# Latencies of tiny DMAs in a planned kernel, earlier float64 conversion, and a float32 attention turned on TensorE

## The chip, the cores and the metric

The kernel runs on one core of a Trainium2 chip. The metric is the device time of one execution in microseconds. The core has TensorE (PE), VectorE (DVE), ScalarE (ACT) and GpSimd (POOL), each running its own instructions in order, and SyncE (SP), which here issues all DMAs, also in order.

## The reference

Clustered attention over 2 batches of 8 heads, 768 positions and 64 channels, then two feed-forward layers over 1536 tokens of 512 channels. All arithmetic of the reference is float32, except that the weights of the first layer, `w_in` and `w_out`, come as float64.

```python
q_assign = np.argmax(einsum('bhsd,hcd->bhsc', q_n, c_n), axis=-1)      # 16 clusters, normalised
k_assign = np.argmax(einsum('bhsd,hcd->bhsc', k_n, c_n), axis=-1)
scores = np.where(q_assign == k_assign, scale * q @ k.T, -1e9)
attn = softmax(scores); x = attn @ v                                   # to 1536 x 512
h = x @ w_in;  g = h * clip(h + 3, 0, 6) / 6;  x = g @ w_out           # 512 -> 2048 -> 512
for e in range(4):                                                     # 512 -> 1024 -> 512 each
    out += p[:, e:e+1] * (maximum(x @ w1[e], 0) @ w2[e])
```

## The kernel before

One batch (half of the tokens) after the other: attention of batch 0, Moe1 of batch 0 (`w_in`, `w_out`, four chunks of 512 hidden channels), Moe2 of batch 0 (`w1`, `w2`, eight chunks) with the attention of batch 1 mixed in, Moe1 of batch 1, Moe2 of batch 1. Every large product is made of half-precision parts: a float32 value is scaled and split into a high and a low float16 half, and three products (`mm3`, L903 to L905) stand for one.

Attention takes two heads at a time (a pair, 4 of them) and 256 queries at a time (a block, 3 per pair). For each 128 queries `scores` makes two products of the queries with the 768 keys (L760, L762), whose second adds the cluster mask; in batch 0 a filling product of `junk` (L758) goes ahead. DVE takes the row maximum (`ut`, L767), ACT the exponential `e` with its sum (L768). `sums` (L776, L777) gives the reciprocal, and `halves` makes the normalised high and low halves `p` on ACT, POOL and DVE (L782 to L791). A DMA (`pt<-p`, L725) turns them, and 18 pairs of float16 products with `vh` and `vl`, the halves of v (L699, L700), make `psv` (L738). ACT and DVE split it into x1h and x1l (L746, L747), the input of Moe1.

`conv_w` converts one chunk of `w_in` or `w_out` from float64 bits to float32 in four steps of 128x512 values. Each step loads 512 KB (`r64`), ACT takes an absolute value (L884), and DVE does L885 (limits, with the maximum), L887, L889 and L891 (shifts and joins of bits). `allmax` then finds the chunk's maximum: DVE reduces to one value per partition (`am`, L503), a DMA writes 128 values to DRAM (`mx<-am`, L506), a second DMA reads them back to all partitions (`bc<-mx`, L508), DVE reduces (L509). `split_w` scales by it and splits into `w` (ACT L808 and L811, POOL L812); the halves are written to DRAM (`hl`) for batch 1. `load_w` does the same for the float32 weights of Moe2, and `vmax` for v. There are 26 such pairs of DMAs. `allmax_pe` does it for activations by a transpose and a product on the PE.

The order of all instructions on all queues is made by a planner in the kernel itself. Each piece of work has an engine, a modelled duration and a due time (`prio`); `plan` goes through modelled time and places on each engine what could start first, then what is due first. A DMA's modelled time is 1.1 us plus its bytes at 360 GB/s, and 0.91 to 1.0 us more until another engine or another DMA may use it. `PAR` holds due times, engine choices and buffer counts. Pools of buffers open and close in groups: the attention's buffers of batch 0 (`g_a[0]`) must close before Moe1's conversion buffers and its second weight pool open. The four buffers of `wrca` and two of `r64a` serve the first chunk, those of `g_m[0]` the other seven.

## Time and profile before

| | us |
|---|---|
| median of 3 runs | 1231.6 (1228.99 to 1234.57) |
| the profiled execution | 1227.56, its span 1225.8 |
| PE busy | 967.3 (79%) |
| DVE busy | 815.6 (67%) |
| ACT busy | 581.4 (47%) |
| POOL busy | 406.4 (33%) |

The shares are means over stages of different kinds. Read the stages first, then the chain of waits in each, then who waits for whom. A stage in which the PE is busy nearly all the time at full clock can only become shorter by less work; in the others one looks for what the waiting engine stands in front of.

### The profile page before, as it was taken

The page shows a single profiled execution, that of the slowest core. Times are in us where ns is not written, and L with a number is a line of the kernel's source. Part 1 is how long each engine was busy: PE and PEld are TensorE (multiplying, and loading weights), DVE is VectorE, ACT ScalarE, POOL GpSimd, SP SyncE. Part 2 cuts the span into 40 slices and gives each one's busy share as a digit, 9 for nine tenths or more (in the row PEclk, how much of TensorE's full clock was granted, in tenths as well). Part 3 has the DMA queues.
Part 4 walks back from the last instruction along what each step waited for, and adds up shares of the span by engine and source line. Part 5 has one row for each costly group of instructions (what it writes and reads, how often), then busy time and mean ns, then how long its engine had stood idle before and what let it go on. Part 6 is the DMA issues. An engine that isn't in the chain of part 4 may idle for free.

```text
span 1225.8 us, 16019 instructions
## 1 busy us (share of the span) xinstructions
PE 967.3 (79%) x5567; PEld 560.6 (46%) x5567; DVE 815.6 (67%) x1644; ACT 581.4 (47%) x1061; POOL 406.4 (33%) x353
## 2 busy tenths in 40 slices
PE   3476773667779577757769677999999989999998
PEld 2355551334345234433435344565566545555554
DVE  9798856549636657745655366666978985665544
ACT  6467762544553344524536244444555454443332
POOL 3566850323551526545434244422000001111111
PEclk9677887798889788878889897999999999999999
DMA  9497798667532557986657295568333314332211
GB/s 270 88 200 136 152 193 237 210 128 192 117 109 76 195 49 160 168 113 166 177 88 192 48 170 102 165 140 182 133 104 103 104 35 138 103 104 70 69 36 52
DMA packets 216562, 161.50 MB, mean 132 GB/s; under 512 B 161505, under 2 KB 164833, under 8 KB 216481
## 3 DMA queue, kind: packets, MB, share of 16 engines
q1 hardware_dynamic: 216480, 160.48, 55.2%
q8 instruction: 43, 0.70, 0.2%
q14 instruction: 39, 0.31, 0.1%
HBM read 86.70 MB, written 31.47 MB: 96 GB/s over the span
## 4 chain that ended last, share of the span: by engine, by line
PE 38%; DMA 30%; DVE 19%; POOL 4%; issue 4%; ACT 4%; SPq 1%; POOLq 0%; ACTq 0%; DVEq 0%
DMA mx<-am 11%; DMA pt<-p 9%; PE psm L903 5%; PE psm L904 5%; PE psm L905 5%; PE psw L981 4%; PE psw L982 4%; PE psw L980 4%; DVE p L791 3%; DMA bc<-mx 3%; DMA wraw<-in_w 3%; PE psg L904 3%; PE psg L905 3%; PE psg L903 3%; PE psv L738 2%
## 5 line engine op out<-in xcount | busy, mean ns | idle before, releaser
L905 PE MATMUL psm<-w,h 128*128 128x512 f16 x384 | 148.3, 386 | 17.8 <-DVE h L1144 9.1
L903 PE MATMUL psm<-w,h 128*128 128x512 f16 x384 | 148.4, 386 | 10.3 <-DVE xv L527 6.3
L904 PE MATMUL psm<-w,h 128*128 128x512 f16 x384 | 148.0, 385 | 0.0
L1144 POOL TENSOR_TENSOR h<-t,h 128x384 f16<-128x384 f32 x32 | 29.1, 916 | 329.9 <-ACT h L1143 309.7
L768 ACT ACTIVATE e<-pss,ut 128x768 f32<-128x768 f32 x96 | 86.0, 897 | 103.1 <-DVE ut L767 35.2
L904 PEld LDWEIGHTS <-w 128*128 128x128 f16 x704 | 71.3, 101 | 118.1 <-issue 79.7
L903 PE MATMUL psg<-g,w 128*128 128x384 f16 x256 | 88.4, 345 | 42.0 <-DVE t L1050 21.3
L903 PE MATMUL psm<-x2h,w 128*128 128x384 f16 x288 | 98.8, 343 | 17.1 <-DVE oa L1169 16.8
L791 DVE SCALAR_TENSOR_TENSOR p<-e,ut,p 128x768 f16<-128x768 f32 x62 | 79.4, 1286 | 37.5 <-POOL p L789 30.8
L738 PE MATMUL psv<-pt,vh 128*64 128x256 f16 x576 | 61.0, 336 | 54.3 <-DMA pt<-p 46.2
L903 PEld LDWEIGHTS <-w 128*128 128x128 f16 x704 | 71.2, 101 | 71.1 <-issue 16.1
L905 PEld LDWEIGHTS <-w 128*128 128x128 f16 x704 | 71.4, 101 | 60.2 <-issue 17.0
L904 PE MATMUL psm<-x2l,w 128*128 128x384 f16 x288 | 98.0, 340 | 0.1
L905 PE MATMUL psm<-x2h,w 128*128 128x384 f16 x288 | 97.5, 339 | 0.0
L1144 DVE TENSOR_TENSOR h<-t,h 128x384 f16<-128x384 f32 x96 | 62.8, 655 | 50.5 <-ACT h L1143 50.4
L767 DVE TENSOR_REDUCE ut<-pss 128x1 f32<-128x768 f32 x96 | 90.0, 945 | 8.0 <-PE pss L762 7.7
L904 PE MATMUL psg<-g,w 128*128 128x384 f16 x256 | 88.2, 345 | 5.7 <-POOL g L1052 2.9
L812 POOL TENSOR_TENSOR w<-wraw,w 128x512 f16<-128x512 f32 x64 | 80.1, 1272 | 34.8 <-ACT w L811 34.3
L1169 DVE SCALAR_TENSOR_TENSOR oa<-psm,pq,oa 128x512 f32<-128x512 f32 x84 | 62.6, 745 | 41.5 <-PE psm L905 41.1
L905 PE MATMUL psg<-g,w 128*128 128x384 f16 x256 | 87.8, 343 | 0.7 <-POOL w L812 0.7
L789 POOL TENSOR_SCALAR p<-e,ut 128x768 f16<-128x768 f32 x49 | 49.1, 1003 | 109.9 <-DMA pt<-p 58.2
L760 PE MATMUL pss<-ka,qa 128*128 128x384 f32 x192 | 71.0, 455 | 10.4 <-ACT e L768 10.3
(191 smaller groups left out, 2317.0 us busy)
## 6 DMA issues: line engine op xcount, KB each, us to landing
wraw<-in_w SPq DMA_DIRECT2D x92, 256.0 KB, 4.5
hl<-w SPq DMA_DIRECT2D x64, 256.0 KB, 4.6
w<-hl SPq DMA_DIRECT2D x64, 256.0 KB, 3.2
r<-in_w_in SPq DMA_DIRECT2D x16, 512.0 KB, 5.2
r<-in_w_out SPq DMA_DIRECT2D x16, 512.0 KB, 6.5
nat<-in_nat SPq DMA_DIRECT2D x16, 384.0 KB, 5.3
raw<-in_qk SPq DMA_DIRECT2D x16, 384.0 KB, 5.1
hl_i<-w SPq DMA_DIRECT2D x16, 256.0 KB, 4.4
```

Of the source, the lines that this page charges most:

```text
L738: nc.tensor.matmul(ps[64 * q:64 * q + 64], vs[vi][:, q, t], pts[q][:, :, pi * NT + t], start=i == 0, stop=i == n - 1)
L760: nc.tensor.matmul(ps[:, f, 0:HS], qa[:, qs], ka[:, f * HS:f * HS + HS], start=True, stop=False)
L767: dve(S, p, lambda: nc.vector.tensor_reduce(out=nb(), in_=ps[:, :, 0:HS], axis=AX.XY, op=ALU.max, negate=True), [ps], [(tb, n)])
L768: act(S, p, lambda: nc.scalar.activation(out=e.t.rearrange("p (a b) -> p a b", a=2), in_=ps[:, :, 0:HS], func=AF.Exp, bias=nb(), scale=1.0 ...
L789: pool(S, p, lambda: nc.gpsimd.tensor_scalar(out=pp[:, j, 0], in0=e.t, scalar1=rs(), scalar2=1.0, op0=ALU.mult, op1=ALU.mult), [e, key], [ ...
L791: dve(S, p, lambda: nc.vector.scalar_tensor_tensor(out=pp[:, j, 1], in0=e.t, scalar=rs(), in1=pp[:, j, 0], op0=ALU.mult, op1=ALU.subtract) ...
L812: pool(512, p, lambda w=w, raw=raw: nc.gpsimd.tensor_tensor(out=w[:, 1], in0=raw.t, in1=w[:, 0], op=ALU.subtract), [raw, (w, 0)], [(w, 1)])
L903: nc.tensor.matmul(o_, ah, bh, start=i == 0, stop=False)
L904: nc.tensor.matmul(o_, ah, bl, start=False, stop=False)
L905: nc.tensor.matmul(o_, al, bh, start=False, stop=i == 3)
L1144: low = lambda e: e.tensor_tensor(out=h[:, 1], in0=t.t, in1=h[:, 0], op=ALU.subtract)
L1169: dve(512, p, lambda: nc.vector.scalar_tensor_tensor(out=oa[:, t], in0=ps.t, scalar=q, in1=oa[:, t], op0=ALU.mult, op1=ALU.add), [ps, qk], ...
```

## The change

1. `add`, `dve` and `dma` take a `lag`, which delays in the plan whoever uses the result. `allmax` gives 7.0 us to the `mx` DMA, 4.0 us to the `bc` DMA and 0.3 us to the small DVE reduction. For v (both batches) the maximum now crosses partitions on the PE, as `allmax_pe` did; that function is merged into `allmax`.
2. `conv_w` is no longer called by Moe1. All eight conversions are recorded with due times from 90 us on, one per 22 us; their buffers (3 of `r64`, 8 of `wrc`, 4 of `stg`) are in a group of their own that is open from the start. The halves are written to DRAM only, and Moe1 of batch 0 reads them back as batch 1 does. Scaling of these weights moves from ACT to POOL.
3. The attention of batch 0 keeps its exponentials in float32. `turned` scales `e` on POOL, transposes it on the PE in two groups of three 128x128 blocks, copies each group out of PSUM (four of five on ACT, one on DVE), and multiplies by v in float32: 6 pairs of products per block. x1h and x1l are scaled as they leave PSUM. There are no halves of p and v, no turning DMA and no filling product in this attention; it has two score buffers in PSUM, where there were three, and two for the transposes.

```diff
-    spc=0.0,
-    cv=0.0,
-    wse=dict(i="A", o="A", **{"1": "P", "2": "A"}),
+    spc=4.0,
+    wse=dict(i="P", o="P", **{"1": "P", "2": "A"}),
+    lr=0.3,
+    ld=(7.0, 4.0),
-    r64p=-11.808027221836664,
+    r64p=6.0,
-    fill=384,
+    fill=0,
+    cv0=90.0,
+    cvd=22.0,
+    cvb=(3, 8, 4),
...
-                x.ready = max(x.ready, end + self.LAT.get((t.eng, x.eng), 0.0) + (0.31 if t.cols < 0 else 0.0))
+                x.ready = max(x.ready, end + self.LAT.get((t.eng, x.eng), 0.0) + (0.31 if t.cols < 0 else 0.0) + t.lag)
...
-    p_s = [Pool("ps_sa", 3, g_pa, True), Pool("ps_sb", 2, g_ps, True)]
+    p_s = [Pool("ps_sa", 2, g_pa, True), Pool("ps_sb", 2, g_ps, True)]
+    p_tr = Pool("ps_ta", PAR["trh"], g_pa, True)
...
-    r64 = [Pool("r64a", 2, g_l0), Pool("r64b", 4, g_m[0])]
-    wrc = [Pool("wrca", 4, g_l0), Pool("wrcb", 9, g_m[0])]
+    p_r64, p_wrc, p_stg = (Pool(x, k, g_cv) for x, k in zip(("r64", "wrc", "stg"), PAR["cvb"]))
...
+    def allmax(am, n, inv, ki, unit, sc, ks, p, bits=False, pp=None):
+
+        dve(n, p, lambda: nc.vector.tensor_reduce(out=am[:, n:n + 1], in_=am[:, 0:n], axis=AX.X, op=ALU.max), [am], [(am, "r")], lag=G["lr"])
+        if pp is None:
...
+            dma(5e3, p, lambda: nc.sync.dma_start(out=dr.t.unsqueeze(1), in_=am[:, n:n + 1]), [(am, "r")], [dr], lag=G["ld"][0])
+            bc = Buf(p_bc, [128, 128], F32, "bc")
+            dma(65e3, p, lambda: nc.sync.dma_start(out=bc.t, in_=dr.t.partition_broadcast(128)), [dr], [bc], lag=G["ld"][1])
...
+        def turned(self, hp, blk, p, avp):
...
+                    e = self.scores(qa, qb, ka, kb, blk * BQ + j * 128, tb, 0, p(i))
+                    self.sums(tb, 1, p(i), 1.0)
+                    sc = lambda eng, e=e, tb=tb: eng.tensor_scalar(out=e.t, in0=e.t, scalar1=tb[:, 2:3], scalar2=1.0, op0=ALU.mult, op1=ALU.mult)
...
+                        pe(NT // nh * 0.109, p(i) + PAR["trp"], turn, [e], [ps], NT // nh * 128)
...
+                        if PAR["kt"][((blk * 4 + i) * nh + h) % len(PAR["kt"])] == "A":
+                            act(S // nh, p(i) + PAR["trp"], lambda src=src, dst=dst: nc.scalar.activation(out=dst(), in_=src(), func=AF.Copy), [ps], [key], ps=True)
+                        else:
+                            dve(S // nh, p(i) + PAR["trp"], lambda src=src, dst=dst: nc.vector.tensor_copy(out=dst(), in_=src()), [ps], [key])
...
+            def av(part):
+                for t in range(part * NT // parts, (part + 1) * NT // parts):
+                    for q in range(2):
+                        nc.tensor.matmul(ps[64 * q:64 * q + 64], vr[:, q, t], pts[q][:, :, t], start=t == 0, stop=t == NT - 1)
...
-            if self.b == 0:
-                conv_w(key, {"i": w_in, "o": w_out}[n][c], p, 0 if (n, c) == ("i", 0) else 1)
-            else:
-                again_w(key, p)
-                if n == "i" and self.wino(c):
-                    sums_w(key, lambda k: wscr[key[1:]][k], p)
+            again_w(key, p)
+            if n == "i" and self.wino(c):
+                sums_w(key, lambda k: wscr[key[1:]][k], p)
...
-            a0.block(hp, blk, lambda i, t0=when[hp, blk]: t0 + i * T_UNIT, G["ka"][hp][4 * blk:4 * blk + 4], G["xba"][3 * hp + blk], G["avp"])
+            a0.turned(hp, blk, lambda i, t0=when[hp, blk]: t0 + i * T_UNIT, G["avpa"])
+
+    for i in range(2 * NC1):
+        n, c = "io"[i % 2], i // 2
+        conv_w((0, n, c), (w_in, w_out)[i % 2][c], G["cv0"] + G["cvd"] * i)
```

On DVE, at the end of the first attention, the kernel before runs as follows (`x1l0` is the attention's last result, `am_2112` the maximum of the first chunk of `w_out`):

```order
L885 TENSOR_SCALAR wconv_2120,am_2112<-wconv_2120 128x512
L747 SCALAR_TENSOR_TENSOR x1l0_820<-psv_2029,x1h0_809 128x256
L891 SCALAR_TENSOR_TENSOR wconv_2110<-r64_2102,wconv_2110 128x512
L887 TENSOR_SCALAR wconv_2120<-wconv_2120 128x512
L885 TENSOR_SCALAR wconv_2133,am_2112<-wconv_2133 128x512
L889 SCALAR_TENSOR_TENSOR wconv_2120<-r64_2104,wconv_2120 128x512
L887 TENSOR_SCALAR wconv_2133<-wconv_2133 128x512
L891 SCALAR_TENSOR_TENSOR wconv_2120<-r64_2104,wconv_2120 128x512
```

Now the same place, with `am_2198` the maximum of the third chunk of `w_out` and `bc_2290` that of the third of `w_in`:

```order
L954 SCALAR_TENSOR_TENSOR wconv_2234<-r64_2177,wconv_2234 128x512
L948 TENSOR_SCALAR wconv_2298,am_2198<-wconv_2298 128x512
L950 TENSOR_SCALAR wconv_2298<-wconv_2298 128x512
L512 TENSOR_REDUCE am_2198<-am_2198 128x1
L952 SCALAR_TENSOR_TENSOR wconv_2298<-r64_2248,wconv_2298 128x512
L954 SCALAR_TENSOR_TENSOR wconv_2298<-r64_2248,wconv_2298 128x512
L764 SCALAR_TENSOR_TENSOR x1l0_783<-psv_2293,vm_67,x1h0_760 128x256
L1110 SCALAR_TENSOR_TENSOR t_2358<-t_2358,psg1_2278 128x384
L519 TENSOR_REDUCE wv_68<-bc_2290 128x1
```

The second of eight conversions was under way when the last `x1l0` was made; now it is the sixth, and its steps are done.

On SP, in the third stage, the kernel before issues one tiny pair per chunk of `w1` or `w2`, among the turning DMAs of the second attention:

```order
L506 DMA mx2252_218<-am_5280 128x1
L725 DMA_TRANSPOSE pt_5455<-p_5487 128x12x128
L508 DMA bc_5530<-mx2252_218 128x128
L725 DMA_TRANSPOSE pt_5536<-p_5517 128x12x128
L725 DMA_TRANSPOSE pt_5536<-p_5552 128x12x128
L506 DMA mx2294_223<-am_5475 128x1
L725 DMA_TRANSPOSE pt_5621<-p_5591 128x12x128
L508 DMA bc_5638<-mx2294_223 128x128
```

Now, at the same kind of place:

```order
L516 DMA mx2445_222<-am_5878 128x1
L886 DMA hl_150_218<-w_5922 128x1024
L893 DMA wraw_5955<-in_w1 128x512
L886 DMA hl_151_219<-w_5931 128x1024
L893 DMA wraw_5978<-in_w1 128x512
L886 DMA hl_152_220<-w_5938 128x1024
L893 DMA wraw_6006<-in_w1 128x512
L886 DMA hl_153_221<-w_6008 128x1024
L893 DMA wraw_6037<-in_w1 128x512
L584 DMA raw_6061<-in_qk 128x768
L584 DMA raw_6063<-in_qk 128x768
L518 DMA bc_6074<-mx2445_222 128x128
```

The `bc` stood two rows behind its `mx`; it stands 11 rows behind it, and the writes and loads of weights go between.

On the PE, in the first attention, the end of one group of scores and the start of a block's products with v stood like this before:

```order
L758 LDWEIGHTS ident_b_61
L758 MATMUL pss_736<-junk_62,ident_b_61 128x384
L760 MATMUL pss_736<-ka_514,qa_498 128x384 x2
L762 MATMUL pss_736<-kb_532,qb_509 128x384 x2
L738 LDWEIGHTS vh_593
L738 MATMUL psv_750<-pt_643,vh_593 64x256
```

Now, with `e` the exponentials that are turned and `vr` the float32 v:

```order
L755 MATMUL psv_716<-pt_599,vr_358 64x256
L755 MATMUL psv_716<-pt_679,vr_358 64x256
L739 MATMUL pst_756<-ident_60,e_650 128x128 x3
L739 MATMUL pst_763<-ident_60,e_650 128x128 x3
L823 MATMUL pss_769<-ka_482,qa_465 128x384 x2
L825 MATMUL pss_769<-kb_502,qb_476 128x384 x2
```

The filling product is gone, a score is followed by six transposes of an earlier row block, and v is read in float32.

## Rows read from the trace of the kernel before

**Rows 1.** Stage windows: us, busy us (count) of five engines, PE clock, DMA share.

```profile
0.00:195.60 195.60, 115.44 (x795) 87.26 (x796) 156.40 (x317) 120.67 (x205) 109.91 (x87) 0.80 0.84 179
27.40:195.60 168.20, 104.80 (x741) 81.70 (x741) 131.85 (x253) 103.02 (x182) 102.40 (x76) 0.77 0.83 159
45.00:110.00 65.00, 39.98 (x270) 31.17 (x270) 60.43 (x110) 41.59 (x73) 41.73 (x29) 0.71 0.83 161
195.60:396.50 200.90, 139.42 (x747) 76.73 (x747) 123.02 (x287) 94.68 (x166) 70.05 (x62) 0.87 0.55 148
396.50:862.00 465.50, 356.36 (x2044) 202.32 (x2043) 287.10 (x547) 204.57 (x380) 197.34 (x172) 0.89 0.67 142
862.00:1225.80 363.80, 356.05 (x1985) 194.28 (x1982) 249.11 (x496) 161.44 (x310) 29.07 (x32) 0.99 0.26 85
```

**Rows 2.** Chain that ended last, from 195.6 to 396.5, then 396.5 to 862.

```profile
by line: DMA mx<-am 32.4%; DMA bc<-mx 8.8%; issue 6.1%; DVE wconv L889 5.8%; DMA r<-in_w_in 5.5%; DVE wconv L891 5.1%; PE psg L904 4.5%; PE psg L905 4.4%; PE psg L903 4.2%; DMA r<-in_w_out 2.7%; DVE wconv L885 2.3%; ACT wconv L808 2.2%; DVE
by line: DMA pt<-p 18.3%; DMA mx<-am 14.3%; DMA wraw<-in_w 7.5%; issue 5.0%; PE psv L738 4.3%; PE psm L903 4.3%; PE psm L904 4.1%; PE psm L905 4.0%; DVE p L791 3.6%; DMA bc<-mx 3.1%; DMA qb<-so 2.7%; POOL p L784 2.0%; DVE am L839 2.0%; POOL
```

**Rows 3.** DMA issues: names, count, KB each, median us to landing.

```profile
bc<-mx SPq DMA_DIRECT2D x26, 64.0 KB, 4.8
mx<-am SPq DMA_DIRECT2D x26, 0.5 KB, 8.5
```

**Rows 4.** Waits: DVE's before 195.6, two of DVE's after it, SP's after 396.5.

```profile
DVE vm L509 <- DMA bc<-mx: 6.4, 1, 6.4
DVE wv L509 <- DMA bc<-mx: 41.7, 7, 9.8
DVE wconv L885 <- ACT wconv L884: 9.5, 3, 4.5
SPq L508 <- DMA mx<-am: 82.3, 14, 9.4
```

**Rows 5.** Timeline of the PE: start us, us, line, tiles, shapes, count.

```profile
75.25 0.85 PE L616 MATMUL psc<-raw,ct 128*32 128x384 f32 x8
...
433.01 0.49 PE L624 MATMUL psct<-ident,sc 128*128 128x128 f32 x3
433.34 0.33 PE L903 MATMUL psm<-x2h,w 128*128 128x384 f16 x1
```

**Rows 6.** Groups by line on DVE, 0 to 195.6: busy us, mean ns, idle.

```profile
L791 DVE SCALAR_TENSOR_TENSOR p<-e,ut,p 128x768 f16<-128x768 f32 x26 | 35.2, 1359 | 9.7 <-ACT p L787 6.4 <-POOL p L789 3.1
L889 DVE SCALAR_TENSOR_TENSOR wconv<-r,wconv 128x512 int32<-128x512 int32 x5 | 5.5, 1091 | 0.0
L887 DVE TENSOR_SCALAR wconv<-wconv 128x512 int32<-128x512 int32 x5 | 4.1, 812 | 0.1
L885 DVE TENSOR_SCALAR_CACHE_REDUCE wconv<-wconv 128x512 f32<-128x512 f32 x6 | 4.0, 673 | 6.7 <-ACT wconv L884 6.7
L891 DVE SCALAR_TENSOR_TENSOR wconv<-r,wconv 128x512 int32<-128x512 int32 x5 | 4.0, 792 | 0.0
```

**Rows 7.** The same from 195.6 to 396.5.

```profile
L889 DVE SCALAR_TENSOR_TENSOR wconv<-r,wconv 128x512 int32<-128x512 int32 x27 | 22.9, 853 | 0.1
L887 DVE TENSOR_SCALAR wconv<-wconv 128x512 int32<-128x512 int32 x27 | 12.5, 465 | 0.2
```

**Rows 8.** ACT's L990; PE's L738 (window 0 to 195.6) and L758.

```profile
L990 ACT ACTIVATE keep<-psw 128x384 f32<-128x384 f32 x20 | 9.8, 488 | 49.4 <-PE psw L982 49.4
0.00:195.60 195.60, 37.00 (x432) 0.80 0.84 179
L758 PE MATMUL pss<-junk,ident_b 128*128 128x384 bf16 x48 | 19.0, 395 | 34.6 <-ACT e L768 34.5
```

**Rows 9.** PE's waits, 195.6 to 396.5 (first), 396.5 to 862 (others).

```profile
PE psg L903 <- DVE t L1050: 32.3, 10, 9.7
PE psv L738 <- DMA pt<-p: 38.5, 10, 7.8
PE pss L762 <- DMA qb<-so: 15.0, 2, 7.6
```

More of the change, by code (lines that the diff above doesn't have):

```diff
@@ L55 @@
     parts=3,
-    ka=["APDPPDPDADPA", "PADPPAPAAPAP", "PPDPPDDAAPAA", "PDPDPDPDPPAD"],
+    avpa=-8.0,
+    kn="PPPPPP",
+    kt="AAAAD",
     kb="DDDP",
@@ L79 @@
     dpx=2,
-    fill=384,
+    fill=0,
+    trp=3.0,
+    trh=2,
+    parta=6,
+    cv0=90.0,
+    cvd=22.0,
+    cvb=(3, 8, 4),
     wo1=0,
@@ L127 @@
 class Task:
-    __slots__ = ("eng", "dur", "fn", "prio", "n", "deps", "succ", "bufs", "ready", "idx", "dma", "cols", "tab", "name", "new", "end")
+    __slots__ = ("eng", "dur", "fn", "prio", "n", "deps", "succ", "bufs", "ready", "idx", "dma", "cols", "tab", "name", "new", "end", "lag")
 class Order:
@@ L155, in group, with add @@
         return g
-    def add(self, eng, dur, prio, fn, reads=(), writes=(), dma=0.0, cols=0, tab=None):
+    def add(self, eng, dur, prio, fn, reads=(), writes=(), dma=0.0, cols=0, tab=None, lag=0.0):
         t = Task()
-        t.cols, t.tab = cols, tab
+        t.cols, t.tab, t.lag = cols, tab, lag
         t.name = (writes[0][0] if isinstance(writes[0], tuple) else writes[0]).name if writes else "out"
@@ L362, in body @@
     NMB = S // MB
+    G = PAR
     o = Order(tc)
@@ L396, in body @@
     g_pf = o.group("psum", after=(g_ps,), keep=True)
-    g_m[0] = o.group("left", after=(g_a[0], g_l0))
+    g_m[0] = o.group("left", after=(g_a[0],))
     g_p0 = o.group("right")
@@ L534, in __init__ @@
             self.b = b
-            self.xb = max(PAR["xba"]) if b == 0 else PAR["xbb"]
-            prep = ("raw", "nat", "vr", "sc", "so", "cs", "oh", "sm")
+            self.xb = PAR["xbb"]
+            prep = ("raw", "nat", "sc", "so", "cs", "oh", "sm") + (("vr",) if b else ())
             P = lambda name: Pool(name + str(b), n[name], gp if name in prep else g)
-            self.p = {k: P(k) for k in ("raw", "nat", "vr", "sc", "so", "cs", "oh", "sm", "e", "p", "pt", "vh", "vl", "tiny")}
+            self.p = {k: P(k) for k in n if k != "stk"}
             if b == 0:
@@ L691, in vmax @@
             k = [(vm, (b, i)) for i in range(3)]
-            allmax(am, NP, vm[:, b, 0:1], k[0], 1.0 / VSC, vm[:, b, 1:2], k[1], p(NP))
-            dve(1, p(NP), lambda: nc.vector.tensor_scalar(out=vm[:, b, 2:3], in0=vm[:, b, 0:1], scalar1=VSC / XSC, scalar2=None, op0=ALU.mult), [k[0]], [k[2]])
+            one = VSC if b else XSC
+            allmax(am, NP, vm[:, b, 0:1], k[0], 1.0 / one, vm[:, b, 1:2], k[1], p(NP), pp=p_tn[b])
+            dve(1, p(NP), lambda: nc.vector.tensor_scalar(out=vm[:, b, 2:3], in0=vm[:, b, 0:1], scalar1=one / XSC, scalar2=None, op0=ALU.mult), [k[0]], [k[2]])
         def values(self, hp, p):
@@ L697, in values @@
             vr, inv, k = st["vr"], vm[:, b, 1:2], (vm, (b, 1))
+            if b == 0:
+                st["v"] = vr
+                return
             vh, vl = self.buf("vh", [128, 2, NT, D], F16), self.buf("vl", [128, 2, NT, D], F16)
@@ L821, in split_w @@
             whl.setdefault(key[1:], []).append(scr)
-            dma(262e3, p + 4, lambda w=w, scr=scr: nc.sync.dma_start(out=scr.t, in_=w.t), [w], [scr])
+            dma(262e3, p + (0 if dst else 4), lambda w=w, scr=scr: nc.sync.dma_start(out=scr.t, in_=w.t), [w], [scr])
     def raw_w(src, p):
@@ L870, in sums_w, with conv_w @@
                 wsum.setdefault(key, []).append(w)
-    def conv_w(key, src, p, which):
-        p -= PAR["cv"]
+    def conv_w(key, src, p):
         am = Buf(p_am, [128, 8], F32, "am")
@@ L877, in conv_w @@
         for k in range(4):
-            r = Buf(r64[which], [128, 512, 2], I32, "r64")
-            raw = Buf(wrc[which], [128, 512], F32, "wconv")
+            r = Buf(p_r64, [128, 512, 2], I32, "r64")
+            raw = Buf(p_wrc, [128, 512], F32, "wconv")
             raws.append(raw)
```

94 lines of the change are left out of this document (60 added, 34 removed).

## The prediction

> **What bounds the kernel now.** I read the busy times by stage first [rows 1]. The cuts are where the work changes: 195.6 us (the first attention's last x1l), 396.5 us (the first Moe1's last product), 862.0 us (the second attention is done); 27.4 us is where the first tiny DMA leaves. After 862.0 the PE is busy 356.05 of 363.80 us at 0.99 of its clock: that stage is PE work, and the change leaves it alone. The three stages before it are not PE bound: 104.80 of 168.20 us at 0.77 (from 27.4), 139.42 of 200.90 at 0.87, 356.36 of 465.50 at 0.89. Next the chain of waits by stage [rows 2]. In the first Moe1, 41.2% of 200.9 us, 83 us, is two tiny transfers: `mx<-am` carries one maximum per partition to DRAM, `bc<-mx` spreads it back. In the third stage they are 17.4% of 465.5 us, 81 us, and `pt<-p`, the DMA that turns probabilities, is 18.3%. The first of the pair lands 8.5 us after its issue in the median, with 0.5 KB, the second after 4.8 [rows 3]. Who pays stands in the waits [rows 4]: DVE stands at L509 for 41.7 us of the first Moe1, and in the third stage the SP queue stands for 82.3 us at L508, the issue of `bc`, with everything behind it unissued. The order explains it: the planner takes some 2 us for such a transfer and puts the reader right behind it.
>
> The first Moe1 has a second trouble: seven of eight float64 conversions lie in it, one in the attention. Its products need little: 139.42 us at 0.87 are 121 us at full clock, with the few that run before 195.6 some 125.
>
> **First attention: what becomes late.** DVE is the busiest engine, 156.40 of 195.60 us [rows 1]. Out go its 26 low halves (35.2), four value splits of the same form (4 x 1.36 = 5.4) and what it converts here now (4.0 + 4.1 + 5.5 + 4.0 = 17.6) [rows 6]: 98 us stay. In come 24 conversion chunks. A chunk is L885, L887, L889 and L891: 0.673 + 0.812 + 1.091 + 0.792 = 3.37 us in this stage [rows 6]; L887 and L889 take 0.465 and 0.853 in the Moe1 stage [rows 7], which makes 2.78. So 67 to 81 us; I take 3.15 a chunk, 76 us, nearer to the row of the same stage. 16 copies out of PSUM at about 0.49 (L990, an ACT copy of that size, is the nearest) [rows 8] are 8 us, the further scale columns some 3. Sum 185 us (176 to 190), of which 156.40 - 131.85 = 24.6 lie before 27.4: 161 us (152 to 166) remain.
>
> The Trainium skill speaks against this part: "GPSIMD Engine Reference", section Specifications, says that GpSimd's SBUF interfaces are shared with VectorE and contend when VectorE runs a two-port mode or has two SBUF inputs. The trace agrees: L887 takes 0.812 us beside a busy POOL and 0.465 beside an idler one. By that rule the chunks cost the upper 81 us, which is in case A below.
>
> DVE's idle time from 27.4 to 195.6 is 36.4 us. 9.7 stood before the low halves that go [rows 6], 6.4 before the maximum of v [rows 4], which now crosses partitions on the PE. 20 us stay, and the attention ends at 27.4 + 161 + 20 = 208 us.
>
> The other engines have room. ACT had 120.67 us; with all of its old work and 80 copies at 0.488 (39 us) [rows 8] it would stand at 160, still under DVE's 185, and it loses two passes over the probabilities. POOL (109.91) gives up its halves' subtractions for 26 more scalings and 32 operations on weights, of a kind that the Moe1 stage ran inside its 70.05 us. On the PE the 48 filling products (19.0) and the half-precision products (37.00) go [rows 8]; 59 us of 115.44 stay. 288 transposes come: three pass in 0.33 us at full clock, before the next product starts [rows 5], so 32 us, and 63 at half clock. And 72 pairs of float32 products of 256 columns come. Their nearest row is L616: eight records, four side by side, of 384 columns in 0.85 us, drain included [rows 5]. Two thirds of that is 0.57, without the drain about 0.45; I take 0.5: 36 us at full clock, 72 at half. Together 127 to 195 us; 160, the middle, fits into 208. The DMA transposes leave the SP queue here.
>
> **First Moe1.** At 208 us six of eight conversions are through DVE. The other two, 8 x 2.78 = 22 us of DVE, are needed after a half and three quarters of the stage, 70 and 105 us later. Weights now go through DRAM and back, 32 writes and 32 reads of 256 KB, each at worst like the tiny pair's 8.5 us [rows 3]; this is free as long as a conversion leads its use by the pair (13 us), its scaling and that round trip (17 us). Only the first read of w_out must wait until the attention's buffers close. The PE's idle time of this stage was 200.9 - 139.4 = 61.5 us. 32.3 of it stood before t, behind a DVE that stood at L509 [rows 9]; that goes. Of the other 29 I keep half, 15: 125 + 15 = 140 us, end at 348 instead of 396.5, **48.5 us** less.
>
> **Second attention and first Moe2.** The instructions stay (only v's maximum moves to the PE); their order changes: most `bc` issues stand 6 to 12 transfers behind their `mx`, where most stood 1 to 5 behind. Full-clock PE work is 356.36 x 0.89 = 317 us of 465.5, so there is room, but something else ends next: `pt<-p`, POOL's halves, the loads of weights. From below the gain is 0: what ends last behind each freed wait may be a transpose. From above it is the chain's 81 us. The PE's own waits lie between [rows 9]: 15.0 us for `qb<-so`, both issued behind a standing SP, and 38.5 us for `pt<-p`, of which I give two thirds, 25, to SP's standing. **40 us.**
>
> **Sum.** The profiled execution took 1227.56 us (span 1225.8). Less 48.5 and 40 it is 1139; the median of the runs, 1231.6, lies 4 us above it: 1143 us.
>
> The Trainium skill's "DMA: Bandwidth & Descriptors", section "Anatomy of one DMA — SWDGE (gpsimd) path", gives a fixed cost of about 2.0 us, on GpSimd's path. By it the planner was right before, the added lags would only put readers late, and the third stage would give nothing, as in case B. Here 0.5 KB from the SP queue take 8.5 us, so the measurement decides for the lags, and B gets no chance from the rule.
>
> **Rivals.** A: DVE keeps today's 78% share of the attention, and chunks cost 3.37: 166 / 0.784 = 212, end at 239, Moe1 at 379, 17.5 us less: 1174. For it: the low halves took 1.359 us in the mean beside POOL [rows 6]; against it: DVE at 93% between 45 and 110 us [rows 1].
>
> B: the third stage gives nothing, since `pt<-p` ends last behind every freed wait: 1183.
>
> C: DVE at 93% with cheap chunks (152 / 0.93, end at 191), Moe1 130 us, and 65 of the 81 us in the third stage: 1091.
>
> D, slower: the PE becomes the bound. It is granted 0.71 where it is busy 62% [rows 1]; if it stays at 1.2 GHz, its 195 us, 184 of them after 27.4, at today's share of 62% take 295: end at 323, Moe1 at 463, 66 us more; 1258 with the 40 us kept. It decides from an attention end of 297 us on, a PE share under 68% at half clock. Against it: the grant rises to 0.87 and 0.89 in the busier stages.
>
> E, not doing what it says: conversions don't run ahead, because three buffers take all float64 loads, and DVE, in order, stands behind each. It stood 9.5 us in 3 such waits [rows 4]; 24 of 3.2 us are 77, end at 285, Moe1 at 425: 1220.
>
> **Chances.** Forecast 0.47, A 0.20, B 0.12, C 0.08, E 0.08, D 0.05. Under 1095 lies half of C, above 1205 D and most of E, so 1095 to 1205 holds 8 in 10. About 0.5% is what a measurement of this kernel can tell from no change. Faster by more: forecast, A, B, C and most of E less their tails, 0.92; within it 0.03; slower 0.05.
>
> **What would show it.** The attention's last x1l between 199 and 215 us with DVE over 85% busy (A: 239; D: a PE over 60% busy at half clock and an end past 297). DVE under 10 us at the reduction of `bc` in the first Moe1, from 41.7. That Moe1's products end near 348 with a PE share over 85% and no wait for weights read back. SP standing under 30 us for `mx` in the third stage, from 82.3, and that stage 425 us long (B: 465). The last stage within 3 us of 363.8. Wrong at the root would be a first attention that ends past 297 us, or a third stage that grows.

## The result, and the profile after

The changed kernel takes 1149.0 us in the median of four runs (1146.42 to 1153.14), the kernel before 1230.3 us beside it: a ratio of 0.934, 95% interval 0.930 to 0.938. The forecast was 1143, with 1095 to 1205 as its range. The profiled execution took 1153.14 us, the slowest of the four; its span is 1151.4.

First the stage windows of the changed kernel: length, then busy us (count) of PE, PE's weight loads, DVE, ACT and POOL, then the granted clock, the share of the DMA engines and GB/s. The cuts are its own, at the same places as in [rows 1].

```profile
0.00:207.80 207.80, 144.65 (x882) 104.03 (x883) 177.71 (x421) 137.15 (x268) 109.52 (x105) 0.89 0.58 153
27.40:207.80 180.40, 135.01 (x834) 99.13 (x835) 154.14 (x360) 120.46 (x247) 103.02 (x95) 0.87 0.53 131
207.80:354.90 147.10, 129.99 (x760) 75.89 (x759) 76.32 (x170) 62.93 (x112) 64.31 (x67) 0.95 0.60 152
354.90:787.00 432.10, 356.54 (x2050) 200.62 (x2049) 289.58 (x551) 205.52 (x380) 195.86 (x172) 0.91 0.75 153
787.00:1151.40 364.40, 354.28 (x1982) 193.57 (x1980) 248.91 (x497) 161.14 (x310) 29.22 (x32) 1.00 0.25 85
```

Against [rows 1] the first attention is 12.2 us longer, the first Moe1 53.8 shorter, the third stage 33.4 shorter, and the last the same within 0.6. The sum is -74.4 us, the difference of the two spans. In Moe1 the PE is now busy 130.0 of 147.1 us, where it was busy 139.4 of 200.9.

The chain that ended last, from 207.8 to 354.9 and from 354.9 to 787, answers to [rows 2]:

```profile
by line: issue 21.1%; PE psg L967 16.3%; PE psg L966 16.3%; PE psg L968 16.0%; DMA bc<-mx 8.5%; DMA scr_i<-wconv 6.9%; DMA w<-hl_i 5.1%; POOL g L1112 4.1%; POOL wconv L873 2.0%; POOL w L875 1.8%; ACT wconv L947 0.5%; PE psm L968 0.5%; ACT t
by line: DMA pt<-p 16.9%; issue 12.6%; DMA wraw<-in_w 8.2%; DVE p L854 5.6%; POOL w L875 4.4%; PE psm L966 4.3%; PE psm L968 4.2%; PE psm L967 4.1%; DVE ut L830 3.3%; PE psv L801 3.1%; DMA vr<-in_vd 2.9%; DVE h L1204 2.8%; DMA kb<-so 2.5%; 
```

`mx<-am`, 32.4% and 14.3% before, is gone from both. Nearly half of Moe1's chain (48.6%) is now the PE's own products, where they were 13% before. But 20.5% of it, 30 us, is three kinds of transfers of moved weights: `bc<-mx`, a write of scaled weights to DRAM (`scr_i<-wconv`), and the read back of split ones (`w<-hl_i`). The transfers themselves are hardly faster, as the DMA issues show (count, KB each, median us from issue to landing; compare [rows 3]):

```profile
bc<-mx SPq DMA_DIRECT2D x24, 64.0 KB, 4.3
mx<-am SPq DMA_DIRECT2D x24, 0.5 KB, 8.5
```

What went is most of the standing in front of them. Waits of the changed kernel (us in total, times, longest): DVE in Moe1, SP in the third stage, then the PE in Moe1, and its largest in the third stage.

```profile
DVE wv L519 <- DMA bc<-mx: 9.8, 2, 6.6
...
SPq L518 <- DMA mx<-am: 8.8, 3, 6.7
...
PE psg L966 <- DVE t L1110: 6.1, 3, 3.4
PE psg L966 <- DVE acc L1136: 5.0, 1, 5.0
PE psg L966 <- ACT acc L1134: 4.6, 1, 4.6
...
PE psv L801 <- DMA pt<-p: 26.1, 8, 7.2
```

DVE stood 41.7 us and SP 82.3 at these two lines [rows 4]; the PE stood 32.3 us for `t` [rows 9]. Over the whole span SP's standing for `mx` at the issue of `bc` falls from 140.8 to 21.8 us, and DVE's for `bc` from 107.1 to 9.8. In the changed kernel SP stands for `mx` for 17.9 us more at other lines, where the kernel before has no such waits.

The first attention pays for what moved into it. Groups of its DVE, PE and ACT work (busy us, mean ns of one, then idle time ahead and what ended it). The copies out of PSUM are 80 on ACT and 16 on DVE, five of six and not four of five on ACT:

```profile
L952 DVE SCALAR_TENSOR_TENSOR wconv<-r,wconv 128x512 int32<-128x512 int32 x24 | 21.7, 908 | 0.0
L954 DVE SCALAR_TENSOR_TENSOR wconv<-r,wconv 128x512 int32<-128x512 int32 x24 | 20.3, 849 | 0.1
L948 DVE TENSOR_SCALAR_CACHE_REDUCE wconv<-wconv 128x512 f32<-128x512 f32 x24 | 16.0, 670 | 7.3 <-ACT wconv L947 7.3
L950 DVE TENSOR_SCALAR wconv<-wconv 128x512 int32<-128x512 int32 x24 | 14.5, 610 | 0.2
L748 DVE COPY pt<-pst 128x384 f32<-128x384 f32 x16 | 8.7, 547 | 2.2 <-PE pst L739 2.2
...
L739 PE MATMUL pst<-ident,e 128*128 128x128 f32 x288 | 49.3, 309 | 33.6 <-ACT pt L746 16.1 <-DVE pt L748 15.4 <-POOL e L727 1.9
L755 PE MATMUL psv<-pt,vr 128*64 128x256 f32 x288 | 38.5, 418 | 0.0
...
L746 ACT ACTIVATE pt<-pst 128x384 f32<-128x384 f32 x80 | 37.1, 490 | 14.0 <-PE pst L739 13.0
```

The 24 conversion chunks are 72.5 us of DVE, 3.02 each; the forecast had 3.15.

### The profile page after: what moved, and what is told of

Same layout as the page of the kernel before. It is cut to its first block, busy times and chain, and to the rows that moved or that the text cites. A ratio compares the mean times of both kernels' runs of the same rounds, so it can differ in the third digit from the quotient of the medians.

```text
span 1151.4 us, 16297 instructions
## 1 busy us (share of the span) xinstructions
PE 985.5 (86%) x5669; PEld 574.1 (50%) x5669; DVE 792.5 (69%) x1636; ACT 566.8 (49%) x1070; POOL 398.9 (35%) x376
## 4 chain that ended last, share of the span: by engine, by line
PE 44%; DVE 19%; DMA 18%; issue 9%; POOL 6%; ACT 3%; SPq 1%; POOLq 0%; ACTq 0%; DVEq 0%
DMA pt<-p 6%; PE psm L966 5%; PE psm L968 5%; PE psm L967 5%; PE psg L966 4%; PE psg L967 4%; PE psg L968 4%; PE psw L1043 4%; PE psw L1045 4%; PE psw L1044 4%; DVE ut L830 3%; DMA wraw<-in_w 3%; DVE p L854 2%; POOL w L875 2%; DMA bc<-mx 1%
## 5 line engine op out<-in xcount | busy, mean ns | idle before, releaser
L831 ACT ACTIVATE e<-pss,ut 128x768 f32<-128x768 f32 x96 | 86.2, 899 | 90.5 <-DVE ut L830 54.1
L1204 DVE TENSOR_TENSOR h<-t,h 128x384 f16<-128x384 f32 x96 | 68.5, 714 | 45.6 <-ACT h L1203 45.4
L966 PE MATMUL psg<-g,w 128*128 128x384 f16 x256 | 84.1, 329 | 3.9 <-DVE t L1110 3.4
L967 PE MATMUL psg<-g,w 128*128 128x384 f16 x256 | 84.2, 329 | 0.9 <-POOL g L1112 0.6
L823 PE MATMUL pss<-ka,qa 128*128 128x384 f32 x192 | 64.1, 417 | 23.5 <-ACT e L831 21.4
L968 PE MATMUL psg<-g,w 128*128 128x384 f16 x256 | 84.1, 329 | 0.0
L739 PE MATMUL pst<-ident,e 128*128 128x128 f32 x288 | 49.3, 309 | 33.6 <-ACT pt L746 16.1
L903 DVE TENSOR_REDUCE am<-wraw 128x1 f32<-128x512 f32 x64 | 42.7, 677 | 50.3 <-DMA wraw<-in_w 50.2
L968 PEld LDWEIGHTS <-h 128*128 128x128 f16 x384 | 38.4, 100 | 69.2 <-DVE h L1204 22.6
```

What stands on the lines that cost most here:

```text
L739: nc.tensor.transpose(ps[:, t // 3, t % 3 * 128:t % 3 * 128 + 128], e[:, x:x + 128], ident.t)
L823: nc.tensor.matmul(ps[:, f, 0:HS], qa[:, qs], ka[:, f * HS:f * HS + HS], start=True, stop=False)
L831: act(S, p, lambda: nc.scalar.activation(out=e.t.rearrange("p (a b) -> p a b", a=2), in_=ps[:, :, 0:HS], func=AF.Exp, bias=nb(), scale=1.0 ...
L966: nc.tensor.matmul(o_, ah, bh, start=i == 0, stop=False)
L967: nc.tensor.matmul(o_, ah, bl, start=False, stop=False)
L968: nc.tensor.matmul(o_, al, bh, start=False, stop=i == 3)
```

## The experiments

The change has three parts: the lags, the early conversions, and the turned attention. v's maximum on the PE is in all kernels made from the changed one (e2 to e5, e8, e10, e11), and of those made from the kernel before (e1, e6, e7, e9, e12) in e9 alone. The runs below take them apart. One table serves all of them. "Attention ends" is the start of its last x1l, Moe1 and the third stage are lengths; their cuts are Moe1's last product and the second attention's last x1l, all read from each trace, so that the third stage ends some 3 us earlier than in [rows 1]. The two columns after that are waits of the whole span: SP at the issue of `bc` for `mx`, DVE at the reduction of `bc` (v's included). SP's waits for `mx` at other lines, up to 18 us in a kernel, are not in the table. Each of its lengths and waits is from one profiled execution. The ratio is to the kernel before on the same chip.

| kernel | median us | ratio (95%) | attention ends | Moe1 | third stage | SP for mx | DVE for bc |
|---|---|---|---|---|---|---|---|
| before | 1228 to 1232 | 1 | 195.1 | 201.3 | 462.6 | 140.8 | 107.1 |
| after | 1149.0 | 0.934 (0.930 to 0.938) | 207.3 | 147.6 | 428.7 | 21.8 | 9.8 |
| e1_lag_only | 1150.2 | 0.937 (0.934 to 0.941) | 175.6 | 190.6 | 415.5 | 26.2 | 6.6 |
| e2_no_lag | 1188.3 | 0.967 (0.963 to 0.971) | 222.7 | 147.2 | 446.0 | 125.5 | 90.5 |
| e3_late_conv | 1149.1 | 0.935 (0.930 to 0.940) | 165.4 | 186.6 | 427.4 | 18.3 | 7.0 |
| e4_old_attention | 1174.2 | 0.957 (0.952 to 0.961) | 230.0 | 158.4 | 420.1 | 6.5 | 4.7 |
| e5_half_early | 1133.9 | 0.923 (0.921 to 0.925) | 197.2 | 141.6 | 426.5 | 11.8 | 1.9 |
| e6_mx_lag | 1166.1 | 0.949 (0.947 to 0.951) | 181.5 | 194.0 | 422.4 | 7.0 | 31.2 |
| e7_bc_lag | 1194.2 | 0.972 (0.969 to 0.974) | 183.2 | 191.0 | 456.2 | 131.7 | 25.1 |
| e8_turned_no_lag | 1200.2 | 0.977 (0.974 to 0.979) | 174.2 | 200.2 | 456.4 | 129.8 | 112.5 |
| e9_vmax_pe | 1226.3 | 0.996 (0.994 to 0.998) | 194.9 | 207.7 | 451.7 | 139.1 | 103.8 |
| e10_load_lag | 1129.0 | 0.918 (0.914 to 0.921) | 197.2 | 141.9 | 417.7 | 9.2 | 2.3 |
| e11_pt_lag | 1131.8 | 0.920 (0.918 to 0.923) | 198.7 | 140.0 | 425.5 | 8.1 | 2.6 |
| e12_lag_twice | 1172.0 | 0.954 (0.951 to 0.957) | 183.0 | 209.4 | 414.9 | 8.7 | 10.1 |

### e1_lag_only: the kernel before with the lags, and nothing else

```diff
-        dve(n, p, lambda: nc.vector.tensor_reduce(out=r(), in_=am[:, 0:n], ...), [am], [(am, "r")])
+        dve(n, p, lambda: nc.vector.tensor_reduce(out=r(), in_=am[:, 0:n], ...), [am], [(am, "r")], lag=0.3)
-        dma(5e3, p, ... in_=r()), [(am, "r")], [dr])
+        dma(5e3, p, ... in_=r()), [(am, "r")], [dr], lag=7.0)
-        dma(65e3, p, ... partition_broadcast(128)), [dr], [bc])
+        dma(65e3, p, ... partition_broadcast(128)), [dr], [bc], lag=4.0)
```

> The kernel before with the lags alone (7.0, 4.0 and 0.3 us; v's maximum still by DMA, old attention, conversions where they were). My theory: the gains of the change are three that add up. The third stage falls from 465 to about 430 us; in the first Moe1 the 41.7 us of DVE standing go, but each of the seven conversions still has its pair of DMAs between its last DVE step and its scaling, and they follow each other on DVE, so that stage falls from 201 to about 180 only: some 1175 us. Rival 'the lags are all of it' (the Moe1's excess was nothing but DVE standing at the pair): 1155 us or less. Rival 'the lags are small' (transposes end last behind each freed wait): 1205 us or more.

Measured: 1150.2. Three constants in the plan, which add no instruction and remove none, are worth nearly the whole change: 78 of 81 us. My theory, in which the lags gave two thirds, falls; the rival that they are all of it holds here for the time, though not for its reason: only 10.7 of the 78 us lie in Moe1 (190.6 against 201.3), 47.1 in the third stage, and 19.5 in the first attention, where neither theory nor rival had any.

### e2_no_lag: the changed kernel without the lags

```diff
-    lr=0.3,
-    ld=(7.0, 4.0),
+    lr=0.0,
+    ld=(0.0, 0.0),
```

> The changed kernel with all three lags at zero. My theory: first attention and first Moe1 lose some 15 us to DVE and SP standing for eight pairs, the third stage is back at about 465 us: some 1200 us. Rival 'the lags are all of it': 1220 us or more. Rival 'the lags are small': 1160 us or less.

Measured: 1188.3, 39 us slower than the changed kernel and still 40 faster than the one before. That is nearest to the theory, 12 us under it: the third stage is not back at 465 us but takes 446.0. Moe1 is as short as with lags (147.2), with six of eight conversions through DVE by then, although DVE still stands 15.1 us at `bc` in it; the first attention and the third stage pay, 15 and 17 us, which is about the 31 us between the two profiled spans. So the two remedies overlap: the early conversions carry the pairs out of Moe1, the lags take the standing out of it.

### e3_late_conv and e4_old_attention: one part taken back, the lags kept

e3 calls `conv_w` from Moe1 as the kernel before does, with its buffers, due times and engines. e4 calls `block` instead of `turned` in the first attention, with the pools that it needs; v's maximum stays on the PE in it.

```diff
 # e3
-            again_w(key, p)
+            if self.b == 0:
+                conv_w(key, {"i": w_in, "o": w_out}[n][c], p, 0 if (n, c) == ("i", 0) else 1)
+            else:
+                again_w(key, p)
...
 # e4
-            a0.turned(hp, blk, lambda i, t0=when[hp, blk]: t0 + i * T_UNIT, G["avpa"])
+            a0.block(hp, blk, lambda i, t0=when[hp, blk]: t0 + i * T_UNIT, G["ka"][hp][4 * blk:4 * blk + 4], G["xba"][3 * hp + blk], G["avp"])
```

> The changed kernel, but with the conversions, their buffers, due times and engines as before the change (one in the attention, seven in the first Moe1, weights kept in place and not read back); lags and the float32 attention stay. My theory: DVE has some 50 us less in the attention, which then ends near 185 us, bound by the PE's turns and the copies; the first Moe1 needs about 180 us again, since seven conversions of 11 us of DVE and a pair of DMAs each lie in it; third stage 430: some 1170 us. Rival 'the lags are all of it': 1150 us, the same as the changed kernel.

> The changed kernel with the first attention as before the change (halves, turning DMAs, three score buffers, filling product); lags and early conversions stay, with 3 instead of 4 buffers for the split weights, since the old attention needs more room. My theory: DVE keeps its 26 low halves and splits of v and gets the conversions on top, some 210 us of work with 20 idle: the attention ends near 235 us, first Moe1 140, third stage 430: some 1180 us. Rival 'the float32 attention is only a swap, and early conversion is what counts': 1155 us or less.

Measured: 1149.1 and 1174.2. Without the early conversions nothing is lost, so e3's theory (1170) falls: its Moe1 is about as long as expected, but the attention ends at 165 us and not at 185. e4's time is near its theory's 1180, with a Moe1 18 us longer than that had it and a third stage 10 us shorter. The first two stages of e3, length and busy times, beside those of after above:

```profile
0.00:165.40 165.40, 133.10 (x891) 96.45 (x892) 126.13 (x300) 123.85 (x246) 77.77 (x78) 0.98 0.34 107
165.40:352.00 186.60, 139.35 (x752) 77.20 (x750) 123.59 (x291) 95.81 (x167) 67.73 (x62) 0.85 0.63 150
```

With late conversions DVE has 51.6 us less to do in the attention, which ends 42 us earlier, and 47.3 more in Moe1, which is 39 us longer; Moe1 ends at 352.0 instead of 354.9. The early conversions move DVE's work from one stage whose length goes with it into another. The turned attention, for its part, is worth 25 us beside early conversions (e4 against after) and 1 us beside late ones (e1 against e3). In e4 DVE has 195.3 us of work in an attention of 230.0: by these lengths, the turned attention only makes room there for conversions that need not be there.

### e5_half_early: four conversions early, four in Moe1

```diff
-            again_w(key, p)
+            if self.b == 0 and 2 * c + (n == "o") >= 4:
+                conv_w(key, {"i": w_in, "o": w_out}[n][c], p, False)
+            else:
+                again_w(key, p)
...
-    for i in range(2 * NC1):
+    for i in range(4):
...
+    p_r64b, p_wrcb = Pool("r64b", 4, g_m[0]), Pool("wrcb", 9, g_m[0])
```

> The changed kernel, with only the first four of eight conversions run ahead (written to DRAM and read back); the other four are done inside the first Moe1, from buffers that open when the attention closes, straight into the weights' buffers. All work stays. In the changed kernel DVE is busy 177 us of the first 207.8 and 77 us of the next 147.6; with all conversions late it is 126 of 165.4 and 124 of 186.6, and both reach the end of Moe1 at about the same time (354.9 and 352.0 us). Theory (DVE is the one that ends last in whichever stage carries the conversions, so an even split is better than either): attention ends at 185 to 192, Moe1 takes 155 to 160, its end lies at 340 to 348, the third stage keeps its 415 to 429: 1130 to 1142. Rival (what ends last up to Moe1's end is the PE with its weights and its waits, whose busy time is the same in all orders, and the split only moves the cut): Moe1's end at 352 to 358, 1147 to 1155.

Measured: 1133.9, 15 us faster than the changed kernel, with intervals that don't meet. The attention ends 5 us later than the theory had it and Moe1 is 13 us shorter, so that it ends at 338.8. Its two stages:

```profile
0.00:197.20 197.20, 143.21 (x894) 103.78 (x895) 159.63 (x383) 134.77 (x265) 106.79 (x106) 0.90 0.54 156
197.20:338.80 141.60, 127.80 (x746) 74.26 (x746) 91.63 (x208) 65.26 (x116) 64.67 (x66) 0.96 0.55 135
```

Three orders of the same kernel (e3, e5, after) have 126, 160 and 178 us of DVE work in the attention, and it ends at 165, 197 and 207: its end goes with DVE's work. In Moe1 they have 124, 92 and 76, and it lasts 187, 142 and 147. Down to 92 us of DVE work Moe1 goes with it, below that with the PE, busy 128 to 130 us in the last two. That DVE itself decides is argued and not shown, since loads and work of ACT and POOL move with it, and DVE is busy 76% of e3's attention and 66% of its Moe1. Four conversions fit under the PE in Moe1 at no price, so these four are better left where they were. Why Moe1 is 6 us longer in the changed kernel, with less to do, shows in part in the two waits of 5.0 and 4.6 us of the PE for `acc`, above. Ahead of the first DVE had stood 6.6 us at the `bc` of a moved conversion, ahead of the second ACT 7.7 us for a load of float64; no wait of the PE in e5's Moe1 is longer than 3.2 us.

### e6_mx_lag and e7_bc_lag: half of the lags

Both are e1 with one of the two lags on the DMAs set to zero: e6 keeps the 7.0 us on `mx`, e7 the 4.0 us on `bc`.

> The kernel before with half of the lags: 7 us on the first transfer of each tiny pair (and 0.3 us on the reduction ahead of it), none on the second. So bc's issue stands late on SP, but DVE's reduction stands where the planner thinks that bc lands, too early. With both lags this kernel took 1150, without 1228. Theory (most of the loss is SP, which stands at bc's issue with all other transfers behind it): SP stands for mx under 40 us in all, DVE at bc 40 to 60 us, 1160 to 1175, so more of the gain than the other half gives. Rival (the loss is DVE, which stands for the pair as a whole, and SP has slack): 1185 or more.

> The kernel before with the other half of the lags: 4 us on bc, none on mx. bc's issue stands early on SP, which waits there for mx; DVE's reduction stands 4 us later than before. Theory (SP's standing is most of the loss): SP still stands for mx 110 us or more, DVE at bc 40 to 60 us, and the time stays at 1190 to 1215. Rival (DVE's standing is the loss): 1175 or less, at the same standing of SP.

Measured: 1166.1 and 1194.2, both as the theory had it, except that DVE stood even less at `bc` (31.2 and 25.1 us). In the third stage the pair settles whose standing costs. Waits of e6 in its third stage, then of e7 in its own; each time SP at the issue of `bc`, then DVE at its reduction:

```profile
SPq L508 <- DMA mx<-am: 1.2, 1, 1.2
...
DVE wv L509 <- DMA bc<-mx: 10.2, 4, 4.7
```

```profile
SPq L508 <- DMA mx<-am: 81.5, 14, 8.3
...
DVE wv L509 <- DMA bc<-mx: 5.9, 1, 5.9
```

In e7 DVE no longer stands in the third stage (5.9 us, and 55.7 in the kernel before with v's pair), SP does as before, and the stage is 6 us shorter. In e6 SP stands 14.6 us for `mx`, counting three other lines too, and the stage is 40 us shorter. At about the same standing of DVE, 67 us less of SP's are worth 34 us. The loss there was SP, with every other transfer of the stage unissued behind it. The table says the same of all fourteen kernels: where SP stands 125 us or more the third stage takes 446 to 463 us, where it stands under 27 it takes 415 to 429. Within each group the lengths still differ by 14 to 17 us at like standing, so a difference of that size between two plans can't be put down to one cause here. Before the third stage it is not SP alone. In e7 Moe1 is as short as in e1 (191.0 and 190.6 us), though SP stands 44.7 us for `mx` in it; what fell there is DVE's standing at `bc`, from 41.7 to 18.3 us. Of e7's 34 us, 22 lie in the first two stages.

### e8_turned_no_lag and e9_vmax_pe: what helps without lags

e8 is e3 with the lags at zero: the turned attention and v's maximum on the PE are what stays. e9 is the kernel before with v's maximum on the PE only.

```diff
 # e9
-            allmax(am, NP, vm[:, b, 0:1], k[0], 1.0 / VSC, vm[:, b, 1:2], k[1], p(NP))
+            allmax_pe(am, NP, vm[:, b, 0:1], k[0], 1.0 / VSC, vm[:, b, 1:2], k[1], p(NP), p_pm[b])
```

> The changed kernel without early conversions (done where the kernel before does them) and without lags: what stays of the change is the turned float32 attention and v's maximum across partitions by the PE. With lags this kernel took 1149, and the changed kernel without lags 1188 against 1228 for the kernel before, so 41 us come from the attention, from v's maximum or from the early conversions. Theory (the early conversions give most of them, since without lags they take the pairs out of the Moe1 whose DVE and SP stand for them): 1208 to 1222, DVE standing at bc 75 us or more, 35 to 45 of it in the first Moe1, which lasts 195 us or more. Rival (the attention and v's maximum give most of them): 1195 or less, with a first attention that ends before 175 us.

> The kernel before with v's maximum taken across partitions by the PE, as the changed kernel does, and nothing else of the change: two of 26 tiny pairs go. The turned attention and this maximum together, without lags, gave 29 us (1200 against 1229), 21 of them by the end of the first attention (174.2 against 195.1). Theory (the attention gives most, since it takes the low halves off DVE and the transposes off SP): the first attention ends at 187 to 194, SP stands for mx 125 us or more, 1216 to 1228. Rival (v's maximum gives most, because DVE stands for it with all of the attention's reductions behind it): the first attention ends at 182 or before, 1212 or less.

Measured: 1200.2, between the two ranges, and 1226.3, in the theory's range, with the attention's end at 194.9 and so hardly moved. Of the 40 us that e2 gains without lags, some 5 come from v's maximum, 24 from the turned attention, and 12 from the early conversions (1200.2 against 1188.3). The attention's part lies in its own stage (174.2 against 195.1), and so does part of what the lags give there (175.6): with both it is 165.4. Why the lags shorten the old attention by 19.5 us, when SP stands only 8.6 us for `mx` in it and DVE 9.8 for `bc`, may show in SP's other waits. First the kernel before up to 195.6 us, then e1 up to 175.6:

```profile
SPq L725 <- DVE p L791: 18.5, 6, 8.7
SPq L508 <- DMA mx<-am: 8.6, 2, 7.5
SPq L881 <- DVE wconv L891: 4.6, 1, 4.6
```

```profile
SPq L725 <- DVE p L791: 6.9, 8, 1.8
SPq L508 <- DMA mx<-am: 4.0, 1, 4.0
```

The longest of these waits, 8.7 us at a turning DMA for a low half, begins while DVE stands at v's pair, and the DMA engines, busy 0.84 of this stage before, are busy 0.96 of it in e1. These waits fall by 20.8 us together, about what the attention gains, but all of SP's waits in the stage fall by 13.3 only (118.9 to 105.6), and e9, which takes v's pair away, does not end the attention sooner. So the cause stays open, and no run takes the waits one by one.

### e10_load_lag and e11_pt_lag: the same remedy for larger transfers

Both start from e5. e10 adds 2.5 us to the loads of raw weights, e11 2.0 us to the turning DMAs of the second attention.

```diff
 # e10, in raw_w
-                [s] if isinstance(s, Buf) else [], [raw])
+                [s] if isinstance(s, Buf) else [], [raw], lag=2.5)
...
 # e11, in block
-                                [pp], [(ptile, j)], dma=1.344 * xb, cols=-1)
+                                [pp], [(ptile, j)], dma=1.344 * xb, cols=-1, lag=2.0)
```

> The kernel with half of the conversions early (1133.9 us), and in the plan 2.5 us more for each load of raw float32 weights: 256 KB, 4.4 us from issue to landing in the median where the planner counts 1.8. DVE stands 48.2 us in 18 waits for them in its third stage, all in its maxima of these loads. Theory (the planner's short estimate costs there what it cost at the tiny pairs): DVE stands for wraw under 20 us, the third stage takes 405 to 420 us instead of 426.5, 1113 to 1128. Rival (DVE, busy 286 of 426 us, has the slack, and nobody waits for what stands behind these maxima): 1129 to 1139, whatever DVE stands.

> The kernel with half of the conversions early (1133.9 us), and in the plan 2.0 us more for each DMA that turns probabilities in the second attention (4.2 us from issue to landing in the median). This transfer is 21% of the chain of waits in the third stage, and the PE stands 28.9 us for it in 10 waits. Theory (the chain goes through the transfer itself, from the scaled probabilities to the product, and the two buffers of turned blocks set the pace, so a later place in PE's order doesn't shorten it): 1128 to 1140, third stage 420 to 432. Rival (as with the tiny pairs, PE stands only because the product is put too early, ahead of other products): PE stands for pt under 15 us, third stage 405 to 420, 1113 to 1128.

Measured: 1129.0 and 1131.8 against 1133.9. Both waits fell to well under half. DVE for the raw weights in e10 (48.2 us in e5), the PE for turned probabilities in e11 (28.9 in e5):

```profile
DVE am L904 <- DMA wraw<-in_w: 14.9, 9, 3.8
```

```profile
PE psv L802 <- DMA pt<-p: 10.8, 6, 3.3
```

The time hardly did. In e11 the third stage takes 425.5 us against 426.5, as its theory had it. e10's profiled execution has 417.7 there and is the fastest of its four; its interval of the ratio still overlaps that of e5, so a gain of some 5 us is likely and not shown. e10's time lies between its theory's range and its rival's. Taking 33 us of DVE's standing away brought some 5 us, where 67 us of SP's brought 34.

### e12_lag_twice: lags that are too long

e12 is e1 with 14.0 and 8.0 us in place of 7.0 and 4.0.

> The kernel before with both lags doubled: 14 us on the first transfer of a tiny pair, 8 us on the second, where 7 and 4 gave 1150 against 1228, with SP standing for mx 26 us in all and DVE at bc 6.6 us. Theory (what counts is that nothing stands behind the pair; a pair that is planned too late costs little, since most are started long before their weights are used): SP stands under 20 us, DVE at bc under 5 us, 1143 to 1158. Rival (the weights that hang on the pairs come late, so the lag has to be the measured one): the PE waits over 45 us for weights in the first Moe1 (24.5 us with the single lags), its end lies past 380 us instead of 366, 1162 or more.

Measured: 1172.0. The theory that too long costs little falls. SP stands 8.7 us, as little as it should, and the third stage is as short as in e1. But Moe1's end is at 392.4 instead of 366.2, as the rival had it; the PE's wait for weights grew less than it said (over 45 us). PE's first wait in Moe1, in e1 and then in e12:

```profile
PE psg L903 <- ACT w L811: 24.5, 2, 22.5
```

```profile
PE psg L903 <- ACT w L811: 37.6, 4, 22.8
```

Of the 26 us, 7 are the attention's, 13 this wait for weights, and 6 more busy time of the PE, granted 0.83 of 2.4 GHz in this stage instead of 0.87. Here the conversions and pairs feed the running stage, and a plan that counts the pair at twice its length starts what hangs on it too late; that this also makes the attention's 7 us is not shown.

## Why the prediction was right in sum and wrong in part

**The terms.** The attention was to end at 208 us by 161 us of DVE work from 27.4 on and 20 idle; it ended at 207.8, by 154.1 and 26.3. That the end is met so closely is luck: the forecast had 7 us too much work and 6 us too little idle time, and the two cancel. Chunks at 3.02 us and copies at 0.547 (0.49 taken) made DVE's part; the low end of the range, 152, was nearer than the middle. The PE's 127 to 195 us were 144.7, with 38.5 for the products that I had at 36 to 72, and ACT was busy 137, not 160. Moe1 was to take 140 us and took 147.1, with 17.1 us of PE idle for the 15 that I left it, and PE work of 130, not 125. The third stage was to give 40 and gave 33.4; the last changed by 0.6. The signs in the list of what would show it came out, but for 7 us of size in Moe1's end and in the third stage: DVE busy 85.5% of the attention, 9.8 us at `bc` in Moe1, a PE share of 88% there and no PE wait for weights read back, SP at `bc`'s issue for 8.8 us in the third stage (18.0 with its waits for `mx` at other lines).

**The step that failed** is the one that this arithmetic hides: the 48.5 us of Moe1 were written as the fruit of moved conversions and their pairs, and the 40 us of the third stage as that of the lags, two terms that add up (e1's expectation says so in as many words). They don't. The lags alone end Moe1 at 366.2 instead of 396.4 (e1), and with the turned attention at 352.0 (e3), earlier than the changed kernel at 354.9. In the prediction's own words the PE stood for `t` "behind a DVE that stood at L509 [rows 9]; that goes": in e1 it falls to 11.8 us, by the lags, with the conversions where they were.

```profile
PE psg L903 <- DVE t L1050: 11.8, 8, 3.9
```

The stage itself is only 10.7 us shorter in e1, and the PE now waits 24.5 us in it for converted weights (L811), where it waited 14.0; the other 19.5 us of Moe1's earlier end are the attention's. The move does take that wait out of Moe1. What the conversions then take out of Moe1, 39 us, they put into the attention, 42. So beside the lags and the turned attention the move gained nothing. I had both numbers, since the attention that grows by 12 us and the Moe1 that shrinks stood in the same sum, but I never asked what the sum is with the lags and without the move.

**The turned attention** was costed as a loss on the PE, to be hidden, and a relief of some 40 us on DVE and of the turning DMAs on SP. Both came (e3 against e1, first attention: PE busy 133.1 and 113.4 us, DVE 126.1 and 153.7), and together they brought 1 us beside late conversions: the turned attention ends Moe1 14 us earlier, 352.0 against 366.2, and the third stage takes 12 us more. The instructions there are the same, the plan is not; among the kernels with lags the old attention goes with third stages of 415 to 422 us and the turned one with 426 to 429 before any further lag. Why stays open.

**The rivals.** A's chunk price of 3.37 us and its 78% did not come. The row behind it, L887 at 0.812 us beside a busy POOL [rows 6] and 0.465 beside an idler one [rows 7], is now L950 at 0.610 with POOL busy 103.0 of 180.4 us. The Trainium skill's "GPSIMD Engine Reference", section Specifications, says that GpSimd shares its SBUF interfaces with VectorE and contends with instructions that run in a two-port mode or have two SBUF inputs. The trace agrees in that L950 is slower beside POOL's work; which of the two conditions it meets, no view shows. Of its 24 instructions in this attention seven had no POOL instruction beside them and took 0.41 to 0.43 us, and each of the nine that took longer, up to 1.99 us, had one beside it for about half of its time or more. The 0.812 from which A was priced is a mean of five that spread as far (0.40 to 1.85). B, in which the third stage gives nothing because `pt<-p` ends last behind every freed wait, did not come: the stage is 33.4 us shorter, and 40 in e6. `pt<-p` is the largest transfer of the chain before and after (18.3% and 16.9%), but e11 shows that a stage in which the PE waits for it 18 us less is not shorter. Of C, the chunks came halfway (3.02 us), but DVE was busy 85% and not 93%, Moe1 took 147 and not 130 us, and the third stage gave half of the 65. D's slow PE did not come: it was granted 0.89 of 2.4 GHz in the attention, and 0.98 in e3. Nor did E in the attention: at L948, where DVE would stand for each load of float64, it stood 7.3 us, not 77; the two conversions left in Moe1 show 13.6 us of it.

On the lags themselves: `mx` lands 7.8 to 8.8 us after its issue in the median of each of the fourteen kernels. The Trainium skill's "DMA: Bandwidth & Descriptors", section "Anatomy of one DMA — SWDGE (gpsimd) path", has about 2.0 us of fixed cost on GpSimd's path; the kernel before planned with about as much, and e1 shows that this price, with that for `bc`, costs 78 us here, on SP's queue and at DVE. Twice the lag costs 22 of them again (e12).

## What to carry to other kernels

In a planned kernel, hold the planner's latency of every small transfer against its measured one, and do it first. A reader that is placed too early costs by what is queued behind it: in the third stage here it cost much on the queue that issues all other transfers and little on DVE, while in Moe1 DVE's standing counted. Too long a latency is wrong as well. When two parts of a change cure the same wait, their gains don't add: price each part as if the other were there, above all one that moves work from a stage into another stage in which the same engine decides, and then try how much of it to move. Half of the move gave the fastest kernels here (e5, and e10 and e11 made from it).
